# A fused attention and gMLP block on one core: a new hand-written order of steps, with c second on SyncE's queue, the query fold ahead of the value shift and late w_sp blocks

## The chip, the core and the metric

The kernel runs on one core of one Trainium2 chip. The metric is the device time of one execution in microseconds (us). The kernel before took 252.75 us, the median of three runs (252.35 to 254.44).

TensorE is written PE below, VectorE DVE, ScalarE ACT, GpSimd POOL; SP is SyncE, which in this kernel only issues DMAs. "ACTq" and "SPq" are the sequencers of ACT and SP, in which their DMA issues stand.

## What is computed

```python
mod = (silu(c) @ w_mod).reshape(1, 6, 1, 448)      # sa, ca, ga, sb, cb, gb
h = layernorm(x) * (1 + ca) + sa
x = x + ga * A(h)        # attention with 16 heads of 28
h = layernorm(x) * (1 + cb) + sb
x = x + gb * B(h)        # gMLP
# A(h): q, k, v = h @ wqkv; phi(t) = [softmax(t @ w_phi), softmax(-t @ w_phi)]
#       kv = phi(k)^T v ; z = sum phi(k) ; o = (phi(q) kv) / (phi(q) z + 1e-6) ; o @ wo
# B(h): z = gelu(h @ w_in); z1, z2 = halves of 896; z2 = layernorm(z2)
#       g = w_sp @ z2 + b_sp ; (z1 * g) @ w_out
```

x has 2048 rows of 448 in bf16; w_sp is 2048 x 2048, w_in 448 x 1792, w_out 896 x 448, w_mod 448 x 2688, and c is one row of 448.

## The kernel before

**Tiles.** The 2048 rows are 16 tiles of 128 rows. The 448 columns are 4 chunks of 112 (CB), so that a head never spans two chunks; the 896 columns of a half of w_in are 7 chunks of 128. PSUM is handed out as three banks of double size (A0, A1, A2) and two single ones (B0, B1); a step that takes a bank waits until all readers of what stood in it are done.

**The order.** `fast_path` defines some sixty small step functions and then runs one string, `ORDER`, word by word (895 words). A word is a step's name, its numbers, the engine behind a slash and the bank behind an @: `SCv:3/G` is value-row chunk 3 on POOL, `kM:0@B0` the key projection of tile 0 into bank B0. Letters stand for engines: V is DVE, S is ACT, G is POOL, Y is SP. No scheduler reorders anything: the order of the words is the order of the instructions on every engine's queue, and an instruction that waits holds back all that is queued behind it on its engine. DMAs share eight completion slots in the order of the words, so that each DMA also waits for the one issued eight DMAs before it.

```python
ENG = {"V": nc.vector, "S": nc.scalar, "G": nc.gpsimd, "Y": nc.sync}
for word in ORDER.split():
    word, _, slot = word.partition("@")
    word, _, en = word.partition("/")
    nm, _, arg = word.partition(":")
```

**The ramp (to about 28 us).** `du:n` is n matmuls of zeros, 128x256, that keep PE busy while loads are on their way (L686). `ct` turns c into columns (L697), `ce` is its silu, `csA` and `ccA` multiply it with the first two sections of w_mod (L721), `esA` and `ecA` bring the results into shift and scale columns (L728, L725). w_phi and the scale are folded into the key and query weights: `FT` transposes a weight on PE (L779), `ET` copies it out (L783, L785), `FS` and `FC` work out the shift row, `PF` multiplies with w_phi (L806) and `EP` writes the folded weight Wk or Wq with the scale applied (L753 on ACT, L757 on DVE). The value weights are not folded: `SHv` works out their shift row from the unscaled rows on PE (L735), then four `SCv` scale the rows in place, one per chunk (L753, L755, L757 for ACT, POOL, DVE; chunk 0 is read out of PSUM with the shift row). LN1 is `l1s` (statistics, L813), `l1e`, `l1r` (reciprocal root on POOL, L821) and `l1a` (the normalised row block, L824). The first four tiles are transposed on PE (`X` L837, `XE`), the others by DMA (`T1`, L829).

**The key stage (about 12 to 54 us).** Per tile: `kM` projects (L847), `kE` and `kF` are exp of plus and minus on ACT (L850), `vM` and `vC` the value rows (L855, L858), `kS`, `kR`, `kP` normalise the features on DVE and POOL (L861, L865, L868) and `kA` adds to the kv sum on PE (L878). `qM` projects two chunks of queries for 512 rows (L902), `qE` and `qF` are their exp (L907). `gr` and `ge` make the gate rows (L913, L916).

**The attention stage (about 54 to 109 us).** Per tile: `nM` multiplies query features with the kv sum (L930), `nX`, `nC`, `nS`, `nT`, `nA` divide (L938 to L956), `T2` transposes by DMA (L829), `wM` is the output projection (L966), `wR` adds x and sums the row, `wQ` sums the squares (L971, L978 on ACT, L973, L980 on DVE), `l2R`, `l2r`, `l2a` are LN2 (L986 to L999), and `T3` transposes the result by DMA into f_hT (L1004). `wN` is `wM` with one more matmul, of x with the identity (L964), so that ACT can read the sum out of PSUM. `dm:9,3` is nine small matmuls of zeros into the num bank (L935). `csB`, `ccB`, `SHw` and `SCw` prepare w_in as before the value weights.

**The gMLP.** `zM` is z2 = h @ w_in per tile (L1010), `zG` its GELU (L1014), `zQ`, `zR`, `zW`, `zN` its layer norm; `yM` and `yG` are z1, transposed, 512 rows a step (L1039, L1042). `W` loads and transposes 8 blocks of w_sp by DMA (L1047). From 139 us on w_sp @ z2 is done in a scheme with sums of blocks that saves products (`tT`, `sS`, `gM`, `P`, `d`, `x`: L1063 to L1106), with the output projection `oM` (L1120), its add `oE` (L1123) and the stores `oD` between. `ld:bsp` loads b_sp. `guard` and `read` test the range of the sums; the general path behind the test is not taken.

Of the kernel before, what the change touches and what calls it, by code (L numbers as in the profile page):

```python
# [486 lines left out]
def fast_path(tc, A_x, A_wqkv, A_w_phi, A_wo, B_w_in, B_w_sp, B_b_sp, B_w_out, c, w_mod, out, flag):  # L487
    nc = tc.nc
    S = A_x.shape[1]
# [77 lines left out]
    wv = aph.tile([P, KC, D], BF, name="f_wv")  # L567
# [281 lines left out]
    def kE(i, s):  # L849
        nc.scalar.activation(out=Er[i % NR][:, s, :], in_=ps["k" + str(i)][:, 0, 0:D], func=ACT.Exp, scale=1.0 - 2.0 * s)  # L850
# [73 lines left out]
    def nM(i, slot):  # L924
        t = ps["n" + str(i)] = bank(slot, "num")
        E = Eq[i // 8]
        o = (i % 8) * P
        for s in range(2):
            for cc in range(4):
                nc.tensor.matmul(t[:, s, cc * 120:(cc + 1) * 120], lhsT=E[0:CB, cc, s, o:o + P],  # L930
                                 rhs=KVbd[0:CB, s, cc, :, :].rearrange("p h d -> p (h d)"), start=True, stop=True)

    def dm(n, i):
        for _ in range(n):
            nc.tensor.matmul(ps["n" + str(i)][:, 1, 480:512], lhsT=zero[:, 0:P], rhs=zero[:, 0:32], start=True, stop=True)  # L935
# [12 lines left out]

# [12 lines left out]
    def wM(i, slot, with_x):  # L961
        t = ps["x" + str(i)] = bank(slot, "x1_ps")
        if with_x:
            nc.tensor.matmul(t[:, 0, 0:D], lhsT=ident[:], rhs=x_sb[:, i, :], start=True, stop=False)  # L964
        for cc in range(KC):
            nc.tensor.matmul(t[:, 0, 0:D], lhsT=oT[0:CB, i % 4, cc, :], rhs=wo_s[0:CB, cc, :], start=(cc == 0 and not with_x), stop=(cc == KC - 1))  # L966
# [261 lines left out]
```

## Time and profile before

| | us |
|---|---|
| median of 3 runs | 252.75 (252.35 to 254.44) |
| the profiled execution | 253.16 |
| its span in the profile | 251.3 |
| PE busy | 241.7 (96%) |
| DVE, POOL, ACT busy | 186.2 (74%), 119.1 (47%), 105.9 (42%) |
| PE idle before its first matmul | 1.24 |
| PE idle in gaps from there to 95 us | 3.9 |
| from the end of the last matmul to the end of the span | about 4 |

The granted clock of PE is full in all 40 slices of the span. An idle time stands in the profile in brackets, before the instruction that ended it, with what released it. The chain of waits is followed back from the last instruction, at each step to what released it, or else to the instruction before it on its engine. A matmul's duration in a row holds its pipelined end, so that neighbouring rows overlap: from one start to the next is its pitch.

### The profile page before, as it was taken

To read this page: it belongs to the slowest core of one execution; us is meant where nothing else is said; L and a number is where in the kernel's file an instruction comes from. 1 tells how busy PE (TensorE), PEld (TensorE's weight loads), DVE (VectorE), ACT (ScalarE), POOL (GpSimd) and SP (SyncE) were. 2 spreads that over 40 slices of the span, in tenths; PEclk is the share of its full clock that TensorE was granted. 3 is DMA by queue.
4 is the path that set the end of the run, shared out by engine and by line. 5 is a ranking of instruction groups with operands and counts; after the bars stand their busy time and mean duration, and the time that the engine had idled before them with its cause. 6 is when DMAs were issued, how large, how long until landed. Compare 5 with 4: busy or idle time off the path is not lost.

```text
span 251.3 us, 4227 instructions
## 1 busy us (share of the span) xinstructions
PE 241.7 (96%) x1550; PEld 127.1 (51%) x1550; DVE 186.2 (74%) x378; ACT 105.9 (42%) x219; POOL 119.1 (47%) x161
## 2 busy tenths in 40 slices
PE   8999998999989799999999999999999999999993
PEld 5865555576546454444444444444444444444451
DVE  4799999777999968874548999599976436644552
ACT  2498977735879658896897300000000000000000
POOL 3749997503568663486834064101119511034530
PEclk9999999999999999999999999999999999999999
DMA  7987569951588849789691977000001000101022
GB/s 181 275 231 173 97 144 200 233 141 21 103 164 113 158 85 183 122 146 221 121 179 28 172 133 77 0 0 0 3 0 37 0 3 1 55 0 37 21 92 68
DMA packets 68208, 25.23 MB, mean 100 GB/s; under 512 B 58129, under 2 KB 67602, under 8 KB 68178
## 3 DMA queue, kind: packets, MB, share of 16 engines
q1 hardware_dynamic: 64848, 20.78, 42.5%
q10 hardware_dynamic: 3330, 4.09, 5.9%
q8 instruction: 14, 0.23, 0.4%
q14 instruction: 16, 0.13, 0.2%
HBM read 8.87 MB, written 1.84 MB: 43 GB/s over the span
## 4 chain that ended last, share of the span: by engine, by line
PE 77%; DVE 11%; DMA 4%; POOL 3%; issue 2%; ACT 1%; POOLq 0%; DVEq 0%
PE g_ps L1085 29%; PE z_ps L1039 10%; PE z_ps L1010 9%; PE o_ps L1120 8%; PE g_ps L1106 5%; DMA f_hT<-f_xpad 4%; PE x_ps L966 3%; PE warm_ps L686 3%; DVE f_st L813 3%; PE q_ps L902 2%; PE v_ps L855 2%; DVE f_ar L950 2%; PE kvacc L878 2%; DVE f_ksum L861 2%; PE num L930 2%
## 5 line engine op out<-in xcount | busy, mean ns | idle before, releaser
L1094 DVE TENSOR_TENSOR f_zb<-g_ps,f_zb 128x512 f32<-128x512 f32 (+1 forms) x31 | 20.3, 669 | 17.5 <-PE g_ps L1085 17.1
L1085 PEld LDWEIGHTS <-f_z2n 128*128 128x128 bf16 x192 | 18.8, 98 | 22.5
L1101 POOL TENSOR_TENSOR f_z1T<-f_zb,f_z1T 128x512 bf16<-128x512 f32 (+1 forms) x11 | 11.9, 1102 | 35.0 <-DVE f_zb L1094 35.0
L1039 PE MATMUL z_ps<-f_hT,f_ar 112*128 112x512 bf16 x112 | 26.3, 379 | 1.3 <-DMA f_hT<-f_xpad 1.3
L1010 PE MATMUL z_ps<-f_ar,f_hT 112*128 112x448 bf16 (+1 forms) x128 | 26.5, 352 | 0.0
L1120 PE MATMUL o_ps<-f_wout,f_z1T 128*128 128x448 bf16 x112 | 22.5, 352 | 0.0
L1085 PE MATMUL g_ps<-f_ar 128*128 128x512 bf16 x96 | 22.2, 379 | 0.0
L1042 ACT ACTIVATE f_z1T<-z_ps,f_zb 128x512 bf16<-128x512 f32 x28 | 18.4, 683 | 6.7 <-PE z_ps L1039 6.7
L1101 POOL TENSOR_TENSOR f_z1T<-f_Sx,f_z1T 128x512 bf16<-128x512 f32 x6 | 7.1, 1182 | 27.2 <-DVE f_Sx L1094 27.2
L907 ACT ACTIVATE f_Eq<-q_ps 112x1024 bf16<-112x1024 f32 x16 | 16.1, 1036 | 6.5 <-PE q_ps L902 6.5
L1010 PEld LDWEIGHTS <-f_hT 112*128 112x128 bf16 (+1 forms) x128 | 12.2, 97 | 11.7 <-DMA f_hT<-f_xpad 0.3
L1039 PEld LDWEIGHTS <-f_ar 112*128 112x128 bf16 x112 | 10.9, 97 | 14.2 <-issue 1.8
L861 DVE TENSOR_REDUCE f_ksum<-f_E 128x32 f32<-128x896 bf16 x16 | 16.7, 1056 | 1.4 <-ACT f_E L850 1.4
L950 DVE TENSOR_TENSOR f_ar<-num,f_w 128x896 bf16<-128x896 f32 x16 | 16.9, 1084 | 0.4
L1014 ACT ACTIVATE f_zb<-z_ps 128x896 bf16<-128x896 f32 x16 | 14.6, 915 | 5.6 <-PE z_ps L1010 4.4
L850 ACT ACTIVATE f_E<-k_ps 128x448 bf16<-128x448 f32 x32 | 16.0, 556 | 1.7 <-PE k_ps L847 1.6
L1085 PE MATMUL g_ps<-f_Eq,f_z2n 128*128 128x512 bf16 x72 | 16.7, 379 | 0.0
L1120 PEld LDWEIGHTS <-f_z1T 128*128 128x128 bf16 x112 | 11.0, 98 | 10.7
L1123 DVE TENSOR_TENSOR f_xpad<-o_ps,f_x 128x448 bf16<-128x448 f32 x16 | 9.9, 621 | 8.0 <-PE o_ps L1120 7.9
L847 PE MATMUL k_ps<-f_Wk,f_hT 113*128 113x448 bf16 (+1 forms) x64 | 14.6, 352 | 0.8 <-DMA f_hT<-f_xpad 0.8
L902 PE MATMUL q_ps<-f_hT,f_Wq 113*128 113x512 bf16 (+1 forms) x64 | 15.0, 379 | 0.1
L1085 PEld LDWEIGHTS <-f_ar 128*128 128x128 bf16 x96 | 9.4, 98 | 11.2
(207 smaller groups left out, 483.1 us busy)
## 6 DMA issues: line engine op xcount, KB each, us to landing
out_dram<-f_xpad SPq DMA_DIRECT2D x16, 112.0 KB, 1.7
f_ar<-in_B_w_in_dram ACTq DMA_DIRECT2D x2, 784.0 KB, 5.3
f_wm<-in_w_mod_dram SPq DMA_DIRECT2D x3, 406.0 KB, 5.8
f_x<-in_A_x_dram SPq DMA_DIRECT2D x2, 448.0 KB, 8.7
f_wmg<-in_w_mod_dram ACTq DMA_DIRECT2D x2, 392.0 KB, 4.2
f_wout<-in_B_w_out_dram SPq DMA_DIRECT2D x1, 784.0 KB, 5.3
f_bsp<-in_B_b_sp_dram SPq DMA_DIRECT2D x1, 512.0 KB, 4.3
f_x<-in_A_x_dram ACTq DMA_DIRECT2D x1, 448.0 KB, 6.3
```

The lines of the kernel that those rows point to most:

```text
L850: nc.scalar.activation(out=Er[i % NR][:, s, :], in_=ps["k" + str(i)][:, 0, 0:D], func=ACT.Exp, scale=1.0 - 2.0 * s)
L861: nc.vector.tensor_reduce(out=ksum[:, i], in_=Er[i % NR][:].rearrange("p s (c f h) -> p (s c) h f", c=4, h=HP), axis=AX.X, op=ALU.add)
L902: nc.tensor.matmul(t[:, u, :], lhsT=Wq[0:KR[m], m, cc * CB:cc * CB + P], rhs=hT[0:KR[m], 4 * st:4 * st + 4, m, :], start=(m == 0), stop=(m ...
L907: nc.scalar.activation(out=Eq[st // 2][0:CB, 2 * c2:2 * c2 + 2, s, (st % 2) * 512:(st % 2 + 1) * 512], in_=ps["q" + str(n)][0:CB, :, :], f ...
L950: nc.vector.tensor_tensor(out=tr[i % 2][:], in0=numv(i)[:, :, :, 0:DH], in1=wr[i // 2 % 2][:, i % 2].unsqueeze(3).to_broadcast([P, 2, H, D ...
L1010: nc.tensor.matmul(t[:, hf, 0:D], lhsT=hT[0:KR[m], i, m, :], rhs=win_s[0:KR[m], m, FH + hf * D:FH + (hf + 1) * D], start=(m == 0), stop=(m ...
L1039: nc.tensor.matmul(t[:, 0, :], lhsT=win_s[0:CB, m, fc * P:(fc + 1) * P], rhs=hT[0:CB, 4 * st:4 * st + 4, m, :], start=(m == 0), stop=(m == ...
L1042: nc.scalar.activation(out=stage_b()["z1T"][:, fc, st * 512:(st + 1) * 512], in_=ps["y%d_%d" % (st, fc)][:, 0, :], func=ACT.Gelu_apprx_tan ...
L1085: nc.tensor.matmul(g, lhsT=sta[:, m, :], rhs=mov[:, m, :], start=(m == 0 and i in (1, 6, 7)), stop=(m == 7), skip_group_check=True)
L1094: nc.vector.tensor_tensor(out=o, in0=x, in1=y, op=ALU.add)
L1101: eng.tensor_tensor(out=z, in0=T[r][:, c0:c1], in1=z, op=ALU.mult)
L1120: nc.tensor.matmul(ps["o" + str(t)][:, 0, 0:D], lhsT=later["z1T"][:, FO[n], t * P:(t + 1) * P], rhs=wout_s[:, FO[n], :], start=(n == 0), s ...
```

## The change

ORDER is written anew, with 893 words; the last 87 (from `P:1,0,x` for the lower half on) are the same. Beside it, `dm` goes, and so does the word `wN`: `wM` takes an engine, and adds the identity matmul where this is ACT.

```diff
-du:2@A1 ld:wk/S ld:x1/Y l1s:1 l1e:1,2/V l1r:1,2 tbl du:3@A2 ld:c/S du:3@A0 m1/G ld:x0/Y ld:wsa/Y m2a/V du:3@B1 du:14@A1 m4 ld:phi/Y du:3@B0 l1s:0 ct@B0
+tbl du:8@B1 m2b/V ld:wk/Y du:3@A2 m2a/V du:11@A1 ld:c/Y ct@B0 ld:x1/S l1s:1 ld:x0/S l1s:0 m1/G ld:phi/Y ce:1 m3 FTk:1@B1 ce:2 l1e:1,2/G ld:wsa/Y du:2@A0
...
-SHv@A1 SCv:0/S EPk:2/V EPk:3/V kM:0@B0 l1a:3/V SCv:2/V FTq:0@B1 ld:x3/Y SCv:1/S ETq:0/V kE:0 FTq:1@A1
...
-SCv:3/G FCq/S EPq:1/S XE:3/S vM:1@A0
+kM:1@B1 FTq:1@A2 ETq:1/V ld:x3/Y FTq:0@B0 ETq:0/V kM:0@A0 kF:1 FSq@A2 FCq/V kE:1 kS:1 PFq:1@B0 scb kF:0 kE:0 l1r:2,4 l1a:2/G l1a:3/G l1s:4 X:2@B1 SHv@A1 PFq:2@A2
+SCv:1/G EPq:1/S XE:2/S l1s:6 PFq:0@B0 SCv:2/G X:3@A0 l1s:5 kM:2@B1 SCv:0/S XE:3/S l1s:7 ld:x4/Y l1s:9 EPq:0/S SCv:3/G l1e:4,8/G l1s:11 kS:0 vM:2@A1 vM:3@B0
...
-    def dm(n, i):
-        for _ in range(n):
-            nc.tensor.matmul(ps["n" + str(i)][:, 1, 480:512], lhsT=zero[:, 0:P], rhs=zero[:, 0:32], start=True, stop=True)
...
-"wM": lambda i, slot: wM(i, slot, False), "wN": lambda i, slot: wM(i, slot, True),
+"wM": lambda i, slot, eng: wM(i, slot, eng is nc.scalar),
```

What moves, by stage (82 steps also change their engine; the new file's line numbers are 43 higher up to L935 and 39 higher behind it):

- **Loads.** On SP's queue: wk, c, phi, wsa, wca, x2, wq, wv, x3, x4, then wmgb and wmga; x1 and x0 stand on ACT's queue. Before, wk and c stood on ACT's queue and x1, x0 first on SP's. x5 now stands on ACT's queue behind the exp of key tile 2; win0 and wout are issued by ACT at the end of the key stage, win1 by SP.
- **Warm-up.** 22 matmuls of zeros ahead of `ct` where there were 28, and 35 in all where there were 41.
- **Ramp.** Key tile 1 comes ahead of tile 0. The query weights are transposed and their fold is begun ahead of `SHv`, which moves behind `kM:0`. Value chunks 1, 2 and 3 are all scaled on POOL (before: ACT, DVE, POOL), and `vM:2` is the first value projection.
- **Attention.** Five tiles take the identity matmul (0, 1, 2, 3, 5) where seven did (0, 1, 2, 3, 4, 10, 11). `SHw:2` moves to where `dm` stood. Four of the `SCw` stand on ACT between the queries' exps, where one did; `nM:13` and the output projections of tiles 10 to 14 come later, that of tile 14 just ahead of `zM:8`.
- **z2 and z1.** `T3:14,16`, the last transpose of LN2's rows, is issued behind more work of POOL and SP. Most blocks `W:1,x` and the load of b_sp move behind `T3:10,12`, six blocks `W:2,x` into the stage with the products, and `yG:2,1` with them; `tT:1,2` moves to POOL and `tT:4,0` to DVE.

Three places show the move. **POOL's queue in the ramp**, from the normalised rows of LN1's first tiles on (f_wv are the value rows, f_xpad normalised rows, f_phik key features). Before:

```order
L824 TENSOR_SCALAR f_xpad<-f_x,f_nm_143,f_rs_142 128x4x112
L755 TENSOR_SCALAR f_wv<-f_wv,f_ca_136 112x448
L673 COPY f_scb<-f_scol 112x512
L817 TENSOR_SCALAR f_rs_142<-f_mv_141 128x4
L818 TENSOR_SCALAR f_nm_143<-f_mv_141 128x4
L821 TENSOR_TENSOR f_rs_142<-f_rs_142,f_mhalf 128x4
L824 TENSOR_SCALAR f_xpad<-f_x,f_nm_143,f_rs_142 128x4x112 x4
L868 TENSOR_TENSOR f_phik<-f_E_123,f_kr_129 128x896
```

and now:

```order
L798 TENSOR_SCALAR f_wv<-f_wv,f_ca_136 112x448 x3
L860 TENSOR_SCALAR f_rs_142<-f_mv_141 128x4
L861 TENSOR_SCALAR f_nm_143<-f_mv_141 128x4
L864 TENSOR_TENSOR f_rs_142<-f_rs_142,f_mhalf 128x4
L867 TENSOR_SCALAR f_xpad<-f_x,f_nm_143,f_rs_142 128x4x112 x4
L911 TENSOR_TENSOR f_phik<-f_E_123,f_kr_129 128x896
```

Three value chunks stand in a row ahead of LN1's next tiles, where one did; the copy of f_scb has gone ahead of them.

**ACT's queue in the attention stage**, from the second exp of query chunk 5 (the first row) to `wR` of tiles 2 and 3 (f_Eq are the exps, f_Sx copies from num, f_ar<-sh_ps and f_ar<-f_ar rows of w_in being scaled, f_x and f_ar<-f_x the steps `wR` and `wQ`). Before:

```order
L907 ACTIVATE f_Eq<-q_ps 112x2x512
L753 ACTIVATE f_ar<-sh_ps,f_cb_83 113x448
L938 COPY f_Sx<-num 128x32
L971 ACTIVATE f_x,f_s_88<-x_ps 128x448
L938 COPY f_Sx<-num 128x32
L978 ACTIVATE f_ar,f_s_89<-f_x 128x448
L971 ACTIVATE f_x,f_s_88<-x_ps 128x448
L978 ACTIVATE f_ar,f_s_89<-f_x 128x448
L907 ACTIVATE f_Eq<-q_ps 112x2x512
L938 COPY f_Sx<-num 128x32 x2
L907 ACTIVATE f_Eq<-q_ps 112x2x512
L971 ACTIVATE f_x,f_s_88<-x_ps 128x448 x2
```

and now:

```order
L950 ACTIVATE f_Eq<-q_ps 112x2x512
L1010 ACTIVATE f_x,f_s_88<-x_ps 128x448
L796 ACTIVATE f_ar<-sh_ps,f_cb_83 113x448
L977 COPY f_Sx<-num 128x32 x2
L1017 ACTIVATE f_ar,f_s_89<-f_x 128x448
L1010 ACTIVATE f_x,f_s_88<-x_ps 128x448
L796 ACTIVATE f_ar<-f_ar,f_cb_83 112x896 x2
L950 ACTIVATE f_Eq<-q_ps 112x2x512
L977 COPY f_Sx<-num 128x32 x2
L796 ACTIVATE f_ar<-sh_ps,f_cb_83 113x448
L950 ACTIVATE f_Eq<-q_ps 112x2x512
L1010 ACTIVATE f_x,f_s_88<-x_ps 128x448 x2
```

Two scalings of 112x896 and a second one of 113x448 have come between the queries' exps; the second `wQ` has gone to DVE.

**SP's queue in the z2 stage**, around the last transposes of LN2's rows (f_hT<-f_xpad are `T3`, f_Eq, f_wsp and f_hT<-in_B_w_sp blocks of w_sp). Before:

```order
L1004 DMA_TRANSPOSE f_hT<-f_xpad 128x8x128
L633 DMA f_bsp<-in_B_b_sp_dram 128x2048
L1004 DMA_TRANSPOSE f_hT<-f_xpad 128x8x128
L1047 DMA_TRANSPOSE f_Eq<-in_B_w_sp_dram 128x8x128
L1004 DMA_TRANSPOSE f_hT<-f_xpad 128x8x128
L1047 DMA_TRANSPOSE f_Eq<-in_B_w_sp_dram 128x8x128 x2
L1004 DMA_TRANSPOSE f_hT<-f_xpad 128x8x128
L1047 DMA_TRANSPOSE f_Eq<-in_B_w_sp_dram 128x8x128
L1047 DMA_TRANSPOSE f_wsp_85<-in_B_w_sp_dram 128x8x128
```

and now:

```order
L1043 DMA_TRANSPOSE f_hT<-f_xpad 128x8x128 x2
L1086 DMA_TRANSPOSE f_Eq<-in_B_w_sp_dram 128x8x128 x3
L1043 DMA_TRANSPOSE f_hT<-f_xpad 128x8x128
L1086 DMA_TRANSPOSE f_Eq<-in_B_w_sp_dram 128x8x128 x3
L1086 DMA_TRANSPOSE f_wsp_85<-in_B_w_sp_dram 128x8x128 x2
L676 DMA f_bsp<-in_B_b_sp_dram 128x2048
L1086 DMA_TRANSPOSE f_hT<-in_B_w_sp_dram 128x8x128 x2
```

Ahead of the last transpose of LN2's rows stand three w_sp blocks where two did, and b_sp has gone from ahead of three of these transposes to behind all of them.

49 lines of the change are left out of this document (45 added, 4 removed).

## The prediction

> **What bounds the kernel now.** I read the busy shares and the chain of waits first, then PE's waits, then stretches of the span.
>
> ```profile
> PE 241.7 (96%) x1550; PEld 127.1 (51%) x1550; DVE 186.2 (74%) x378; ACT 105.9 (42%) x219; POOL 119.1 (47%) x161
> PE 77%; DVE 11%; DMA 4%; POOL 3%; issue 2%; ACT 1%; POOLq 0%; DVEq 0%
> 98.00:139.00 41.00, 41.00 (x204) 19.51 (x203) 27.69 (x77) 33.99 (x68) 24.97 (x44) 1.00 0.73 138
> 139.00:188.00 49.00, 49.00 (x229) 22.21 (x228) 43.28 (x55) 2.42 (x4) 11.94 (x6) 1.00 0.31 49
> ```
>
> PE is the bound: 77% of the chain is its own, and in the stretches from 98 to 188 us (columns: length, then busy time of PE, of its weight loads, DVE, ACT, POOL, the granted clock, the DMA share, GB/s) it is busy in every microsecond. There a new order gains nothing; it can only lose. What can be gained is PE work left out and PE's waits, and these are few:
>
> ```profile
> PE z_ps L1039 <- DMA f_hT<-f_xpad: 1.3, 1, 1.3
> PE warm_ps L686 <- DVE f_zero L644: 1.2, 1, 1.2
> PE num L930 <- DVE f_ar L950: 1.2, 3, 0.6
> PE k_ps L847 <- DMA f_hT<-f_xpad: 0.8, 1, 0.8
> PE num L930 <- ACT f_zb L1014: 0.7, 1, 0.7
> ```
>
> (Columns: total, times, longest.) The wait for zeros opens the program and stays. The other four, 3.9 us by their gaps, lie between 42 and 95 us, three of them in the attention stage. Together with the PE work removed below they are nearly all that the change can win.
>
> **The start.** c is issued second on SP's queue, where x0 was; x1 and x0 take the first places on ACT's, which wk and c had, so that all four are issued within the same first microsecond as before and cost nothing.
>
> ```profile
> 1.24 5.24 PE L686 MATMUL warm_ps<-f_zero 128*128 128x256 bf16 x28 [1.24 <-DVE f_zero L644]
> 6.53 0.31 PE L697 MATMUL ct_ps<-f_one,f_c_row 1*112 1x1 bf16 x4
> 1.24:3.24 2.00, 2.00 (x10) 1.44 (x11) 1.00 0.63 144
> 7.87:8.76 0.89, 0.89 (x8) 0.68 (x8) 1.00 1.12 275
> 5.62 0.63 DVE L813 BATCH_NORM_STATS2 f_st<-f_x 128x6 f32<-128x448 bf16 x1
> 7.30 0.58 POOL L821 TENSOR_TENSOR f_rs<-f_rs,f_mhalf 128x1 f32<-128x1 f32 x1
> 10.96 0.16 DVE L725 TENSOR_SCALAR f_ca<-cf_ps 112x4 f32<-112x4 f32 x1
> 12.71 0.55 PE L847 MATMUL k_ps<-f_Wk,f_hT 113*128 113x448 bf16 x2
> ```
>
> The first warm-up matmuls come at 2.00/10 = 0.20 us each, later ones at 0.89/8 = 0.11. Of the 28 ahead of `ct` the last six go, and these are of the later kind: 6 x 0.11 = 0.65 us, so that `ct` could start at 5.9 instead of 6.53. Charged at the mean of the first row (5.24/28 = 0.19) it would be 1.1 us. The Trainium skill, "TensorE: Matmul & The Clock Gate", section "What's actually happening", has the warm-up last for a time (some 3.4 us) and not for a number of matmuls; the two rates above agree, and by it too the six that go are cheap ones. Little of the 0.65 reaches the key projection. x0 is now transposed first; its statistics can't begin before it lands (5.6 in the DVE row), and behind the root on POOL (7.30 + 0.58 = 7.9) and the row block on DVE (0.39) it is ready at about 8.3, where PE arrives at 7.9 (two sets of transposes at 0.46 and eight warm-ups from 5.9 on). From there X, csA, PF, X, FS and ccA bring the scale column to about 10.5 (10.96 in the row), and the last of three folds of Wk in a row on ACT, at the pitch of 0.53 that two rows below have, is done at about 12.4. Key tile 1 then ends at 12.6, where before tile 0, with the value shift done too, ended at 12.71 + 0.76 = 13.47. The shift's 0.76 is still to do: I take **-0.2 us**.
>
> **The value rows.** The four chunks are needed by the first value projection.
>
> ```profile
> 11.95 0.92 PE L735 MATMUL sh_ps<-f_wv,f_Ga 112*128 112x448 bf16 x4
> 12.91 0.63 ACT L753 ACTIVATE f_wv<-sh_ps,f_ca 113x448 bf16<-113x448 f32 x1 [0.33 <-PE sh_ps L735]
> 13.44 0.66 ACT L753 ACTIVATE f_wv<-f_wv,f_ca 112x448 bf16<-112x448 bf16 x1
> 13.08 1.08 POOL L755 TENSOR_SCALAR f_wv<-f_wv,f_ca 112x448 bf16<-112x448 bf16 x1
> 13.35 0.39 DVE L824 TENSOR_SCALAR f_xpad<-f_x,f_nm,f_rs 128x448 bf16<-128x448 bf16 x1
> 20.04 2.80 POOL L824 TENSOR_SCALAR f_xpad<-f_x,f_nm,f_rs 128x448 bf16<-128x448 bf16 x4
> 20.03 0.63 DVE L813 BATCH_NORM_STATS2 f_st<-f_x 128x6 f32<-128x448 bf16 x1
> ```
>
> Before, ACT, DVE and POOL shared them, and all were scaled 2 us ahead of need. Now chunks 1 to 3 follow one another on POOL behind `SHv`. PE issues, from the end of `SHv` to `vM:2`, two PF (0.21 each), an X (0.23) and `kM:2` (0.76), 1.4 us, and meets chunk 3 another 0.57 later: cover of 2.0 us. POOL's rows give two prices for such a block of 448: 2.80/4 = 0.70 while DVE ran statistics, 1.08 once, while DVE ran a scaling out of SBUF. Three in a row are 2.1 or 3.2 us, and with the hand-over (some 0.2) the stall is 0.4 or 1.4. DVE's queue beside the three holds statistics and a sum over features, so I take 0.70 and **+0.4**, and keep +1.4. Queued behind these on POOL are LN1's tiles 4 to 7, which the fifth key tile needs 8 us later: covered.
>
> **The key stage.** k_ps waited 0.77 us for the transposes of tiles 12 to 15. Their LN1 rows on POOL and DVE come earlier among the words than the key tiles that use them did, so I take all of it, **-0.77**, and keep 0 (x5 is issued later, behind `kF:2`).
>
> **The attention stage up to the first z2 tile.** The nine small matmuls go, and of seven identity matmuls two.
>
> ```profile
> L964 PE MATMUL x_ps<-f_x,f_ident 128*128 128x448 bf16 x7 | 2.5, 353 | 0.0
> 67.09 0.38 PE L935 MATMUL num<-f_zero 128*128 128x32 bf16 x9
> 70.03 0.59 PE L930 MATMUL num<-f_ar,f_Eq 112*128 112x120 bf16 x8 [0.61 <-DVE f_ar L950]
> 54.00:78.00 24.00, 22.77 (x233) 13.73 (x231) 20.05 (x51) 16.86 (x41) 12.42 (x20) 1.00 0.48 91
> 65.18 0.63 ACT L753 ACTIVATE f_ar<-sh_ps,f_cb 113x448 bf16<-113x448 f32 x1 [0.32 <-PE sh_ps L740]
> 81.04 1.04 ACT L753 ACTIVATE f_ar<-f_ar,f_cb 112x896 bf16<-112x896 bf16 x1
> 66.67 0.58 ACT L978 ACTIVATE f_ar<-f_x 128x448 bf16<-128x448 bf16 x1
> 76.40 1.04 ACT L907 ACTIVATE f_Eq<-q_ps 112x1024 bf16<-112x1024 f32 x1
> ```
>
> `dm` is 0.40 by its row. It stood in front of a num that then waited 0.61 for DVE: taken out alone it would only lengthen that wait, but `SHw:2` (four matmuls, 0.76) moves into its place. So **-0.40**, and the three waits of num for DVE, 1.2 together, go by the order of the tiles if nothing else is late: **-1.17**. PE's lead at the first z2 tile would be 0.2 - 0.4 + 0.77 + 0.40 + 1.17 = 2.1 us.
>
> It meets ACT there. `zM:0` takes the bank of the last query chunk and waits for its second exp, 76.40 + 1.04 in the row. Ahead of it ACT now has two scalings of 1.04 and one of 0.63 more, and one square (0.58 and 0.18 for reading its sum out) less: 2.71 - 0.76 = 1.95 us. From 54 to 78 us ACT idled 24.00 - 16.86 = 7.1 us, so all of it could be hidden; but most of that idle time ends with PE's queries, ahead of the added scalings, and those stand in front of exps that other work waits for. I take the pessimistic end, **+1.95** (0 at the other), a lead of 0.2 at `zM:0`.
>
> **Behind it.** The wait of z_ps for a transpose (1.31) was for LN2's rows of tiles 2 and 3. In the new order PE has 5.4 us of work from `zM:0` to that use, and ACT's squares, POOL's moments and root and the transpose need about 5.7 from there: **-1.0**. The one num that now takes a bank behind a GELU (tile 15) has two z1 steps, 1.7 us, of cover: **-0.68**. Two identity matmuls at a pitch of 0.19 (448 columns each, as the k_ps rows: 0.76 for four): **-0.38**. A new wait: `nM:13` takes the bank of the output projection of tile 8, and DVE reads that only behind a division and two adds.
>
> ```profile
> 73.24 2.08 DVE L950 TENSOR_TENSOR f_ar<-num,f_w 128x896 bf16<-128x896 f32 x2
> 75.35 0.39 DVE L956 TENSOR_TENSOR f_ar<-f_ar 128x448 bf16<-128x448 bf16 x1
> 80.00 0.61 DVE L973 SCALAR_TENSOR_TENSOR f_x<-x_ps,f_x 128x448 bf16<-128x448 f32 x1
> ```
>
> On DVE 1.04 + 2 x 0.39 + 0.7 = 2.5 us, on PE two projections and a num, 1.9: **+0.6** (0 to 1).
>
> **The z2 stage and the products.** The last transpose of LN2's rows is the one that comes late.
>
> ```profile
> 108.20 1.68 PE L966 MATMUL x_ps<-f_ar 112*128 112x448 bf16 x8
> 126.01 2.75 PE L1039 MATMUL z_ps<-f_hT,f_ar 112*128 112x512 bf16 x12
> 122.67 1.23 SPq L1004 DMA_TRANSPOSE f_hT<-f_xpad  x1
> 120.00 1.07 DVE L980 SCALAR_TENSOR_TENSOR f_ar<-f_zb 128x896 bf16<-128x896 bf16 x1
> f_hT<-f_xpad SPq DMA_TRANSPOSE x15, 3.3
> ```
>
> Before, 18 us lay between the projection of tile 14 and the first z1 step that needs it. Now PE has six z2 tiles at 1.52, four z1 steps at 0.86 and the guard between them, 12.65 us. DVE's queue there is the read and the two squares of tiles 14 and 15 (2.1), the moments (0.75), one normalised z2 tile (0.5), a square of 896 (1.07) and the two row blocks, about 6.5 with the waits; with 3.3 for the transpose 10 to 12 us. It fits: **0**, up to +2 where POOL's root stands behind zR, zW and zN. The load of b_sp now has some 7 us to its use and took 4.3; the blocks `W:2,x` are used more than ten us behind their place; the last 87 words are the same: 0 each.
>
> **The sum.** -0.2 + 0.4 - 0.77 - 0.40 - 1.17 + 1.95 - 1.0 - 0.68 - 0.38 + 0.6 = -1.65 us, so that the profiled 253.16 us (251.3 of span, 1.9 around it) would be 251.5. It lies 0.4 above its runs' median; for the median, 252.75 - 1.65 = **251.1 us**.
>
> **The rivals.** *All gaps close.* ACT's idle time swallows the scalings and `nM:13` comes in time: -1.65 - 1.95 - 0.6 = -4.2, 248.5 us. For it: 7.1 us of idle; against it: three engines would have to be in time at every tile.
>
> *ACT sets the pace* (the other side). If ACT's queue ends last not only at `zM:0` but on to 98 us, as its GELUs, squares and scalings stand in one line, then the work taken from PE and the waits of the attention stage give nothing, since PE would wait for ACT in their place: -0.2 + 0.4 - 0.77 + 1.95 + 0.6 = +2.0, 254.7 us. It decides once the second exp of query chunk 7 ends more than about 0.5 us later than its 77.4 of now. Against it: ACT's 16.86 busy us in 24.
>
> *The late transpose.* If POOL's root holds the row blocks of tiles 14 and 15 up by 2 us beyond the cover, PE stands in the stage that has no gap now: -1.65 + 2.0, 253.1 us.
>
> *POOL and DVE in each other's way.* The row of 1.08 is 0.38 longer than 0.70, just what the DVE scaling within it took (0.39). If that recurs for all three value chunks: -1.65 + 1.0, 252.1 us. The Trainium skill, "SBUF — State Buffer", section "Who interferes with whom", has DVE's copies and scalings out of SBUF, but not its sums over features, able to lock POOL out for a whole instruction; by that the rows above agree, and the case turns on what DVE runs at that moment.
>
> **How the numbers follow.** My sum 0.40, all gaps close 0.22, ACT 0.20, late transpose 0.10, POOL 0.08. The likeliest alone would give 249.4 to 252.6 (the middle of the ACT term to the upper price of the value rows). The range of 8 in 10 reaches into the ends on both sides: 248.2 to 254.8. One per cent, 2.5 us, is about what a measurement of this kernel can tell from no change. Faster than 250.2: the low three tenths of the sum (0.12), all gaps (0.22), a fourth of POOL (0.02), 0.36. Slower than 255.3: four tenths of ACT (0.08), a fifth of the transpose (0.02), 0.10. Within: 0.54.
>
> **What would show it.** PE's first `ct` near 5.9; an idle piece of 0.3 to 0.6 before the first v_ps, released by POOL; none before k_ps at 42; the second exp of query chunk 7 near 77.3 and z_ps released by ACT there; no num waiting for DVE by more than 0.2 before it; PE full from 98 to 188 us of now, all of it 1 to 2 us earlier. I am wrong if PE shows a gap over 1 us behind 98 us, if the value rows cost over 1 us, or if the gaps of the attention stage come back under new releasers.

## The result, and the profile after

| | before | after |
|---|---|---|
| median, us | 253.59 of 4 (252.35 to 254.44) | 249.31 of 4 (248.69 to 250.34) |
| profiled execution, us | 253.16 | 249.40 |
| its span, us | 251.3 | 247.6 |
| PE busy, us | 241.7 | 240.5 |

The ratio is 0.985, with an interval of 0.9813 to 0.9888: 1.5% faster. A second set gave 249.51 (6 runs, 249.09 to 250.47) against 253.2: 0.9857 (0.983 to 0.9885). The forecast had the sign and the bound, and the time lies within its range (248.2 to 254.8), but of 3.76 us between the two profiled executions it foresaw 1.65, and 249.31 lies just below the 249.4 to 252.6 of its likeliest case.

First the busy shares and the chain of waits of the page after:

```profile
PE 240.5 (97%) x1533; PEld 126.8 (51%) x1533; DVE 182.5 (74%) x369; ACT 104.8 (42%) x217; POOL 116.3 (47%) x175
PE 85%; POOL 6%; ACT 3%; DVE 2%; DMA 1%; issue 1%; POOLq 0%
```

DVE's share of the chain fell from 11% to 2%, PE's rose from 77% to 85%. PE's waits after (columns: in total, times, longest):

```profile
PE warm_ps L729 <- DVE f_zero L687: 1.2, 1, 1.2
PE q_ps L945 <- ACT f_Eq L950: 0.6, 1, 0.6
PE x_ps L1005 <- DVE f_x L1012: 0.3, 1, 0.3
PE g_ps L1145 <- DVE f_z2n L1072: 0.2, 1, 0.2
PE warm_ps L729 <- DVE f_Wk L800: 0.2, 1, 0.2
```

All four waits that the prediction listed are gone, the one for a transpose included (z_ps, 1.31). New are 0.58 for ACT early in the queries, 0.26 for DVE (x_ps), 0.24 within the products (g_ps) and 0.24 in the ramp (warm_ps, for DVE's work on a key weight). The same in stretches from milestone to milestone, first of before, then of after (length, then PE busy and its matmuls):

```profile
54.08:77.64 23.56, 22.32 (x229) 1.00 0.47 89
77.64:139.41 61.77, 59.78 (x332) 1.00 0.74 135
139.41:236.34 96.93, 96.93 (x458) 1.00 0.18 33
```

```profile
53.23:75.55 22.32, 21.72 (x222) 13.29 (x219) 19.18 (x51) 17.66 (x40) 8.73 (x17) 1.00 0.48 119
75.55:134.87 59.32, 59.06 (x330) 29.87 (x329) 43.00 (x110) 47.66 (x103) 40.88 (x81) 1.00 0.80 142
134.87:232.38 97.51, 97.27 (x458) 44.52 (x456) 68.90 (x95) 1.87 (x4) 27.22 (x17) 1.00 0.23 41
```

The stretches end at the first queries behind the kv sum, the first z2 tile, the first product and the last output projection. Against the terms of the sum:

| stretch | forecast | measured |
|---|---|---|
| start to the first of these queries | -0.57 | 54.08 to 53.23: -0.85 |
| to the first z2 tile | +0.38 (of it ACT +1.95) | 23.56 to 22.32: -1.24 |
| to the last output projection | -1.46 | 158.70 to 156.83: -1.87 |
| tail | 0 | 14.96 to 15.22: +0.26 |
| all | -1.65 | -3.70 |

The third row's pieces add up to it: -1.31 (z_ps), -0.68 (num behind a GELU), two identity matmuls at 0.19, and +0.26 and +0.24 for the new waits, -1.87. That they fit so well is partly chance: the stretch ahead of the first product is 0.34 shorter than its pieces say (61.77 to 59.32), the one behind it 0.34 longer (96.93 to 97.51). The second is the row in which the forecast failed: with ACT's term at 0 and the new wait of 0.58 its terms give -0.99, and the rest is a little less PE work (22.32 to 21.72, of which `dm` has 0.40).

### The profile page after: what moved, and what is told of

Its sections match the earlier page's. It is cut to its first block, busy times and chain, and to the rows that moved or that the text cites. A ratio compares the mean times of both kernels' runs of the same rounds, so it can differ in the third digit from the quotient of the medians.

```text
span 247.6 us, 4188 instructions
## 1 busy us (share of the span) xinstructions
PE 240.5 (97%) x1533; PEld 126.8 (51%) x1533; DVE 182.5 (74%) x369; ACT 104.8 (42%) x217; POOL 116.3 (47%) x175
## 4 chain that ended last, share of the span: by engine, by line
PE 85%; POOL 6%; ACT 3%; DVE 2%; DMA 1%; issue 1%; POOLq 0%
PE g_ps L1124 29%; PE o_ps L1159 9%; PE z_ps L1049 7%; PE q_ps L945 6%; PE k_ps L890 5%; PE v_ps L898 5%; PE g_ps L1145 5%; PE z_ps L1078 4%; PE x_ps L1005 4%; PE kvacc L921 3%; PE warm_ps L729 3%; PE num L973 2%; POOL f_zv L1035 1%; DMA f_hT<-f_xpad 1%; DVE f_z2n L1072 1%
## 5 line engine op out<-in xcount | busy, mean ns | idle before, releaser
L1140 POOL TENSOR_TENSOR f_z1T<-f_Sx,f_z1T 128x512 bf16<-128x512 f32 x6 | 8.0, 1332 | 39.3 <-DVE f_Sx L1133 39.3
L1159 PEld LDWEIGHTS <-f_z1T 128*128 128x128 bf16 x112 | 11.0, 98 | 10.7
L1005 PE MATMUL x_ps<-f_ar 112*128 112x448 bf16 x64 | 14.1, 352 | 0.3 <-DVE f_x L1012 0.3
```

The source lines that it names most:

```text
L1140: eng.tensor_tensor(out=z, in0=T[r][:, c0:c1], in1=z, op=ALU.mult)
L1159: nc.tensor.matmul(ps["o" + str(t)][:, 0, 0:D], lhsT=later["z1T"][:, FO[n], t * P:(t + 1) * P], rhs=wout_s[:, FO[n], :], start=(n == 0), s ...
```

## The experiments

All of them are compared with the kernel before on the same chip, whose median was 253.2 in each set.

### One part of the order at a time

**The new order up to the end of the key stage, the old one behind it** (h_abb). ORDER is cut at `KV:0`; a few words that would stand twice or be missing (loads and blocks of w_sp, and the like) are put where their own order has them. The next two are made in the same way.

```diff
 # ORDER, cut at KV:0; ahead of it the new words
-KV:0/V KV:1/V KZ:0 ld:win0/S qM:3@A2 KZ:1 nM:0@A1 qE:3
+KV:0/V KV:1/V qM:3@A2 KZ:0 KZ:1 nM:0@A1 wos:1/V qE:3
...
```

> The new order up to the end of the key stage (all words ahead of KV:0), the old order behind it. Stage-by-stage theory: PE is the bound and each stage's gain is its own, so the first query projection behind the kv sum (q_ps at 54.1 before, 53.2 in the new order) starts near 53.2, the rest is as before: 0.9 us faster than before, span about 250.4. Rival, the lead is lost again: the attention stage of the old order waits for VectorE and transposes, so an earlier start is given back there; then the time is that of before within 0.3 us, with longer waits of num. Rival, the stages gain only together: no gain at the seam either.

Measured: 252.16 (10 runs, 251.83 to 253.49), 0.9974 (0.9953 to 0.9995). The queries start at 53.47, 0.61 earlier than before, and the three waits of num for DVE are back with 1.2 in all. z_ps waits 0.86. The ramp and the key stage alone are worth about 1 us, of which 0.45 is that shorter wait of z_ps, behind the cut.

**The old order up to there, the new one behind** (h_baa).

```diff
 # ORDER, cut at KV:0; ahead of it the old words
-KV:0/V KV:1/V qM:3@A2 KZ:0 KZ:1 nM:0@A1 wos:1/V qE:3
+KV:0/V KV:1/V KZ:0 ld:win0/S qM:3@A2 KZ:1 nM:0@A1 qE:3
...
```

> The old order up to the end of the key stage, the new order behind it. Stage-by-stage theory: q_ps behind the kv sum near 54.1 as before, then the new order's 22.3 us to the first z2 tile (23.6 before) and 59.3 to the first product (61.8 before): 2.8 us faster than before, span about 248.5. Rival, the new attention order needs the lead that the new ramp gives: less than half of that, with waits of num or z_ps that the new order did not show.

Measured: 251.78 (10 runs, 251.02 to 253.57), 0.9964 (0.9941 to 0.9987). From the first queries to the first z2 tile it takes 22.32 us (54.52 to 76.84), just as the whole new order does, so this stretch's gain is that of its own words. But 1.4 us of gain in all is half of the 2.8 expected. PE's timeline shows two waits, both for DMA transposes:

```profile
42.73 0.93 PE L890 MATMUL k_ps<-f_Wk,f_hT 113*128 113x448 bf16 x4 [0.99 <-DMA f_hT<-f_xpad]
83.34 1.02 PE L1082 MATMUL z_ps<-f_hT,f_ar 112*128 112x512 bf16 x4 [0.94 <-DMA f_hT<-f_xpad]
```

The first is 0.2 longer than before; the second stands in words that are the same as in the new order, which has no wait at this place (80.94 in its row below). The two halves are worth 1.04 + 1.42 = 2.46 us, the whole 253.2 - 249.51 = 3.69. Most of the gap of 1.2 can be placed in the traces. Of z_ps's wait the halves take 0.45 and 0.37, the whole takes 1.31: 0.49 is missing. The queries start 0.61 earlier in h_abb and 0.44 later here (0.23 of it by k_ps), 0.85 earlier in the whole: 0.68 is missing.

**Only the words from the first z2 tile on** (h_bba). In it x is added twice in tile 4 and not in tile 5.

```diff
 # ORDER, cut at zM:0; ahead of it the old words, then one more wR
-zM:0@A2 nA:7/G l2R:2,4/G SCw:3,0/V wR:4/S gt nS:4 nT:9
+wR:5/S zM:0@A2 gt nA:7/G l2R:2,4/G nC:9 nS:4 nT:9 nT:8
...
```

> The old order up to the first z2 tile, the new order behind it (the steps done on one side only of the seam are kept once). Stage-by-stage theory: z2 starts near 77.6 as before, and 59.3 us later the products start (61.8 before), less 0.6 that the products lose: 1.9 us faster than before, span about 249.5. Rival, the waits that are gone there (z_ps for a transpose 1.31, num for the GELU 0.68) were set by work ahead of the first z2 tile: they come back, and the gain is about 0.4, the two identity matmuls.

Measured: 252.42 (10 runs, 251.33 to 253.38), 0.9961 (0.9935 to 0.9987). The stretch to the first product takes 60.1 us, between 61.77 and 59.32: z_ps does not wait, but x_ps waits 0.67 and 0.29 for DVE. So this part gives some 0.8, less than the 1.9 expected and more than the rival's 0.4, and the attention stage, h_baa less h_bba, some 0.6, with the 0.94 that h_baa's z_ps waits counted against it.

### The disputed term: does ACT have room?

**The three scalings back on DVE** (scw_back).

```diff
-SCw:2,1/S qM:6@A2 SCw:0,0/S
+SCw:2,1/V qM:6@A2 SCw:0,0/V
...
-SCw:0,2/S qF:6
+SCw:0,2/V qF:6
```

> The new order with three scalings of w_in's rows (chunks 0,0, 2,1 and 0,2) back from ScalarE on VectorE, where they were before; 1.56 us of VectorE, 2.7 us of ScalarE. Theory now: in the old order VectorE paced the attention stage (num waited for it three times), and the gain there is that ScalarE does these rows in its idle time. Then waits of num for VectorE come back and z2 starts 0.5 to 1.5 us later than in the new order (75.6). The recorded sum (ScalarE's added work on the path, +1.95): z2 starts earlier, by 0.6 (its one wait of q_ps for ScalarE) up to 2 us. Third, both have room: within 0.2 us.

Measured: 253.4 (10 runs, 253.22 to 254.29), 1.0019 (1.0 to 1.0038): the whole gain is gone. PE's timeline, and DVE's just ahead of it:

```profile
71.18 0.59 PE L973 MATMUL num<-f_ar,f_Eq 112*128 112x120 bf16 x8 [1.59 <-DVE f_ar L989]
72.18 0.98 PE L973 MATMUL num<-f_ar,f_Eq 112*128 112x120 bf16 x8 [0.41 <-DVE f_ar L989]
```

```profile
67.71 0.81 DVE L800 TENSOR_SCALAR f_ar<-f_ar,f_cb 112x896 bf16<-112x896 bf16 x2 [0.81 <-PE sh_ps L783]
68.44 0.92 DVE L984 TENSOR_TENSOR f_dn<-f_cr 128x32 f32<-128x32 f32 x1
```

On DVE the two scalings take only 0.81, but they wait another 0.81 for `SHw:2`, and the division of the next tiles is queued behind them. The waits of num for DVE are back, 2.0 us of them. Moving these blocks to ACT is what let the waits of num close. The first z2 tile starts at 80.43, 4.5 later than in the new order's second profile, where 0.5 to 1.5 was expected. The waits are 2.0 of it, the queries' later start 0.7 (54.30), and some 1.7 (half of 3.4) comes from the granted clock, which in this execution was halved for 3.4 us there (see the end). Runs with a mean clock of 0.998 to 1.000 took 253.3 to 253.8 too, so that the clock does not carry the loss. Where those spent what the waits don't explain no profile shows.

**More work on ACT** (act_plus): four copies of 128x448 ahead of `qF:6`, nothing depends on them.

```diff
+    def aj(n):
+        for _ in range(n):
+            nc.scalar.activation(out=junk[:, 0:D], in_=junk[:, 0:D], func=ACT.Copy)
...
-SCw:0,2/S qF:6
+SCw:0,2/S aj:4 qF:6
```

> The new order with four added copies of 128x448 on ScalarE ahead of the second exp of query chunk 6, some 1.9 us, as much again as the new order put there. Theory now: in the new order ScalarE runs without idle time from 66 us on and ends the last exp at 75.48, when z2 starts at 75.55; the added 1.9 us come out at the first z2 tile almost whole (77.0 to 77.5) and at the end (1.5 to 1.9 us slower than the new order). Rival, that ScalarE with 42% of the span busy has room: less than 0.5 us. Had the recorded term (+1.95 for the first 1.95 us on this queue) been right, ScalarE would have been late already and the whole 1.9 would come out again, with z2 waiting for ScalarE.

Measured: 253.36, the median of nine runs (252.01 to 254.33; a tenth, at 511 us, is left out), 0.9999 (0.9972 to 1.0025). ACT's row of the copies and PE's row behind them:

```profile
71.34 2.42 ACT L979 ACTIVATE f_ar<-f_ar 128x448 bf16<-128x448 bf16 x4
```

```profile
74.72 2.27 PE L946 MATMUL q_ps<-f_hT,f_Wq 113*128 113x512 bf16 x8 [2.09 <-ACT f_Eq L951]
```

PE takes nearly all of the copies as a wait: the exp behind them ends at 74.68 and releases it. The first z2 tile starts at 80.65, where 77.0 to 77.5 was expected; a halved clock has a part in this as well (see the end). That ACT had no room left shows in the new order too, by its ACT rows:

```profile
73.39 1.00 ACT L950 ACTIVATE f_Eq<-q_ps 112x1024 bf16<-112x1024 f32 x1
74.30 0.26 ACT L977 COPY f_Sx<-num 128x32 f32<-128x32 f32 x2
74.44 1.04 ACT L950 ACTIVATE f_Eq<-q_ps 112x1024 bf16<-112x1024 f32 x1
```

and PE's:

```profile
75.55 1.69 PE L1049 MATMUL z_ps<-f_ar,f_hT 113*128 113x448 bf16 x8
80.94 1.03 PE L1078 MATMUL z_ps<-f_hT,f_ar 112*128 112x512 bf16 x4
```

The last exp ends at 75.48 and the z2 tile that takes its bank starts at 75.55, with no wait. The change filled ACT's idle time to the brim and not beyond. Two stretches of the new order, 66 to 72 and 72 to 78 us (PE, its loads, DVE, ACT, POOL), say the same:

```profile
66.00:72.00 6.00, 5.98 (x43) 3.25 (x41) 5.72 (x14) 5.95 (x13) 4.57 (x9) 1.00 0.41 78
72.00:78.00 6.00, 6.00 (x50) 3.61 (x49) 5.76 (x14) 5.86 (x15) 5.47 (x11) 1.00 0.50 98
```

PE, DVE and ACT are each busy for 5.7 or more of 6 us. The one experiment puts 1.6 us of scaling and waiting back on DVE, the other 2.4 us on ACT, and either loses what was won.

### Where the transpose's wait went

The wait of z_ps for a transpose was 1.31 before, 0.94 in h_baa and none after, though LN2's words are the same in the last two. The next five runs look for what decides it.

**The new order again** (after_again), for a second profile.

```diff
 # no edit
```

> The new order once more, on the chip of the variants of it that follow: about 3.8 us faster than before (ratio 0.985 so far), first z2 tile near 75.5, the products near 134.9.

Measured: 249.51 (6 runs), 0.9857 (0.983 to 0.9885); the queries start at 53.58, the first z2 tile at 75.90, and z_ps does not wait.

**28 warm-ups ahead of `ct`, as before** (du28).

```diff
-tbl du:8@B1 m2b/V
+tbl du:14@B1 m2b/V
```

> The new order with the six warm-up matmuls back, 28 ahead of ct. If warm-up matmuls are plain TensorE work on the path, 0.65 us slower than the new order at the first key projection. But x0's statistics and root set the first transpose (xt_ps at 8.5 in all runs of the new ramp, with or without an idle time ahead of it): then TensorE is later only by what exceeds that, 0.3 to 0.6 us where the clock rises late and nothing where it rises early.

Measured: 250.7 (4 runs, 250.47 to 251.4), 0.9899 (0.9867 to 0.993), 1.2 more than the new order beside it. In the profiled execution (span 249.3 against 247.8) the queries are 0.34 later, as expected (53.92); what was not expected is the wait of z_ps, which is back with 1.30. The DMA view from 79.4 to 82 us (40 slices of 0.065 us) shows a transfer that stops:

```profile
GB/s 32 126 449 224 209 209 197 209 205 169 138 43 24 8 0 0 0 0 0 0 0 0 0 0 0 0 0 4 8 8 8 12 8 8 12 8 12 8 12 59
q8 instruction: 1, 0.02, 3.9%
```

In the new order, from 78.7 to 80.5 (slices of 0.045 us), it runs through:

```profile
GB/s 6 85 148 199 228 210 222 222 233 199 222 210 222 193 222 239 182 228 199 210 210 188 199 228 182 199 199 217 154 80 51 34 370 0 0 0 0 0 0 0
q8 instruction: 1, 0.02, 4.2%
```

In both stretches one packet of 16 KB lies on the queue called "instruction", of which the span has 14. It is the one slice above 300 GB/s (370 GB/s over 0.045 us are 16.6 KB). In du28 it comes 0.1 us after the transfer began, and from 0.85 us after its start the transfer all but stands still (0 to 12 GB/s) for 1.6 us. In the new order it comes at the transfer's end, 1.4 us after its start, and nothing stands still. My theory from here on: these packets come with the number of PE's instructions, and one that comes early in a transpose delays it by a microsecond or more. The rival: the later start of du28 decides.

**Six small matmuls in a wait of PE, at no cost in time** (fetch_early): `dm` again, 128x32, ahead of `qM:4`, where PE waits for ACT anyway.

```diff
+    def dm(n, i):
+        for _ in range(n):
+            nc.tensor.matmul(ps["n" + str(i)][:, 1, 480:512], lhsT=zero[:, 0:P], rhs=zero[:, 0:32], start=True, stop=True)
...
-nT:0 qM:4@A2
+nT:0 dm:6,1 qM:4@A2
```

> The new order with six more matmuls of 128x32 zeros (into unused columns of a num bank) just ahead of qM:4, where TensorE waits 0.58 us for ScalarE anyway; at 0.04 each they cost no time there. They only push what TensorE still has to fetch as instructions by twelve places. Theory: the 16 KB instruction packets on queue q8, one about every 27 us of TensorE work, stop a DMA transpose that is under way for 1.2 to 1.6 us; in the new order such a packet comes at 80.8, just after the transpose of LN2's tiles 2 and 3 has landed. Here it comes some 1.3 us earlier, into that transpose: z2 still starts near 75.6 to 75.9, the first z1 step waits 0.7 to 1.4 us for a DMA as it did before the change, and the time is 0.7 to 1.3 us above the new order's. Rival, that the transpose was late for another reason (the later start of the whole): no wait, the new order's time.

Measured: 250.86 (5 runs, 250.18 to 251.96), 0.9897 (0.9855 to 0.994). The first z2 tile starts at 75.88, as in after_again (75.90), and still:

```profile
82.41 1.02 PE L1082 MATMUL z_ps<-f_hT,f_ar 112*128 112x512 bf16 x4 [0.96 <-DMA f_hT<-f_xpad]
```

Its packet comes 0.75 us after the start of the transfer.

**28 warm-ups ahead of `ct`, but six fewer behind** (du28_same): the count of matmuls at the attention stage is that of the new order again.

```diff
-tbl du:8@B1 m2b/V
+tbl du:14@B1 m2b/V
...
-l1a:0/G du:6@A2 X:0@B0
+l1a:0/G X:0@B0
```

> 28 warm-up matmuls ahead of ct as in the earlier run, but without the six later ones (du:6), so that TensorE has as many instructions ahead of the attention stage as the new order. That earlier run was 1.2 us slower, of it 0.34 in the ramp and 1.30 in a wait of the first z1 step for a DMA transpose. Theory of the instruction packets: the place of the packet is that of the new order again, no such wait, and the time is within 0.4 us of the new order's (249.3 to 250.0). Rival, that the later start of all that follows made the wait: the ramp is as late as in the earlier run and the wait of about 1.3 stays, 250.7.

Measured: 249.97 (5 runs, 249.34 to 251.19), 0.9873 (0.9831 to 0.9914); the first z2 tile at 75.76, and no wait:

```profile
81.16 1.03 PE L1078 MATMUL z_ps<-f_hT,f_ar 112*128 112x512 bf16 x4
```

The packet is at the end of the transfer, 1.4 us after its start. Both runs came out as the theory said. du28_same does not test the rival by itself, as its start was not late (queries at 53.44). fetch_early does: its z2 starts when that of the new order does, and the wait is there. And two runs in this document start z2 late without that wait: h_bba at 77.47 and mended, below, at 77.21; their packets come 2.6 us behind the issue of the transpose, as the new order's does. So the rival falls.

**The old order without `dm`** (old_late), which should bring the packet of the old order late enough.

```diff
-nS:2 dm:9,3 SCw:0,0/V
+nS:2 SCw:0,0/V
```

> The old order without its nine matmuls dm (0.40 us of TensorE). As plain TensorE work they are worth nothing: num waits for VectorE right behind them, 0.61 now and 1.0 then, and z2 starts at 77.6 as before. By the theory of the instruction packets it is worth 0.7 to 1.3 us all the same: nine pairs of instructions fewer bring the packet that came at 81.0, within the transpose of tiles 2 and 3, to about 82.6, when the transpose is through, and the wait of the first z1 step (1.31) goes or shrinks: span 250.0 to 250.6. Rival without such packets: span 251.2 to 251.4.

Measured: 254.55 (11 runs, 253.07 to 256.28), 1.0045 (1.0015 to 1.0074): slower. As forecast, `dm` taken out alone gives nothing: num waits 1.04 in its place, and the stretch up to the first z2 tile takes 23.56 us as before. But z_ps still waits 0.89, so the gain hoped for there is missing. The DMA view from 83 to 85 us (slices of 0.05 us; the transfer began at 82.1) has the reason:

```profile
GB/s 205 543 184 184 138 169 220 164 88 31 0 0 36 72 36 15 15 20 5 0 10 5 10 10 5 10 10 10 10 10 10 5 10 10 10 31 241 276 297 287
```

The packet (543) comes at 83.1, 4.0 us behind the first z2 tile (79.07), where it was 2.7 behind it before: it did move, by 1.3, but it is still only 1.0 into the transfer, which then stops from 83.5 to 84.7. The mechanism stands; how far the packet had to move was misjudged. The ramp, whose words are unchanged, was slower: 28 warm-ups took 6.01 us (5.24 before), and the queries started at 55.51. In this execution the warm-up matmuls go at 6 to 7 a microsecond up to 7.2 us, where before they did so up to 5.2; but the median of eleven runs is slower too, and why is open.

### Two mendings

**Two new waits mended at once** (mended), 0.58 of q_ps and 0.24 within the products: the work of `FB` into the wait of q_ps, with win1 loaded earlier for it, and `tT:1,2` on POOL behind the z2 rows of tiles 14 and 15.

```diff
-csB@B0 W:0,1 ld:win1/Y
+csB@B0 esB W:0,1
...
-nT:0 qM:4@A2
+nT:0 FB@B0 qM:4@A2
...
-nX:3 FB@B1 wos:1/V
+nX:3 wos:1/V
...
-zQ:14/S tT:1,2/G yG:3,0
+zQ:14/S yG:3,0
...
-zR:14,16/G zW:14,16 zN:14/V
+zR:14,16/G zW:14,16 tT:1,2/G zN:14/V
```

(`ld:win1/Y` now stands behind `kF:15`, and `esB` behind `csB`.)

> The new order with its two remaining waits in the middle taken on: the bias matmuls FB (0.68 us of TensorE) go ahead of the query projection that waits 0.58 for ScalarE's exp, with what they need (win1 loaded behind kF:15, the shift column esB right behind csB), and GpSimd's moments of tiles 14 and 15 go ahead of tT:1,2 (2.1 us), which held up the last normalised z2 tiles (0.24). Theory (TensorE is the bound, ScalarE just in time at the first z2 tile): the second gives 0.24; the first gives 0.58 at the query projection, but ScalarE's queue up to the first z2 tile gains only what the earlier query brings it, so 0.3 to 0.6 in all at the products, 0.4 to 0.8 us. Rival: ScalarE's and VectorE's queues are the pace there, and only the 0.24 shows.

Measured: 250.29 (6 runs, 249.55 to 251.19), 0.9886 (0.9857 to 0.9916), 0.8 more than the new order beside it. PE's waits:

```profile
PE x_ps L1003 <- ACT f_zb L826: 1.3, 1, 1.3
PE fb_ps L789 <- DMA f_ar<-in_B_w_in_dram: 0.6, 1, 0.6
```

The 0.58 for ACT became 0.59 for win1's load, and `FB` in bank B0 made the next user of that bank wait for ACT's copy of it, which stands behind exps. The wait of 0.24 within the products did go. Where a gain of 0.4 to 0.8 was expected, 0.8 is lost.

**Only the second of the two** (mended2).

```diff
-zQ:14/S tT:1,2/G yG:3,0
+zQ:14/S yG:3,0
...
-zR:14,16/G zW:14,16 zN:14/V
+zR:14,16/G zW:14,16 tT:1,2/G zN:14/V
```

> The new order with only the second of the two edits tried: GpSimd's moments of tiles 14 and 15 ahead of tT:1,2. The wait of the products for the last normalised z2 tiles (0.24) goes, as it did there; 0.2 to 0.3 us faster than the new order, too little for the timing to tell, to be seen in the places of the rows.

Measured: 249.01 (5 runs, 248.72 to 251.14), 0.985 (0.9802 to 0.9897). The stretch from the first product to the last output projection is 96.93 us again:

```profile
135.07:232.00 96.93, 96.40 (x448) 44.59 (x456) 68.39 (x93) 1.87 (x4) 25.50 (x16) 1.00 0.23 42
```

It is the best of all the kernels here, but its 0.3 to 0.5 below the new order's medians can't be told from them by the times; the stretch in the trace (97.51 to 96.93) is what shows the gain.

## Why the prediction was right, and where its sum failed

**What bounds the kernel: right.** PE did, and its waits between 42 and 95 us were what could be won. All closed; the new ones sum to 1.3 us, and none is over 0.6.

**The start, -0.2: near.** `ct` starts at 6.04 (forecast 5.9). x0 is indeed the next to be late: the first transpose starts at 8.53 (8.3), and the key projection at 12.10 against 12.71. That `ct` came out so near is in part luck: the 22 warm-ups took 3.86 to 4.88 us in the profiles (see the end).

**The value rows, +0.4: none.** POOL's row and the first value projection of the new order:

```profile
16.07 1.87 POOL L798 TENSOR_SCALAR f_wv<-f_wv,f_ca 112x448 bf16<-112x448 bf16 x3 [0.25 <-PE sh_ps L778]
```

```profile
17.58 1.69 PE L898 MATMUL v_ps<-f_wv,f_hT 113*128 113x448 bf16 x8
```

Three scalings take 1.87, 0.62 each (priced 0.70), while DVE runs a sum over features until 16.30 and statistics behind it; v_ps does not wait. (The prediction's own terms, 2.1 + 0.2 - 2.0, give 0.3 and not 0.4.) The price of 1.08 for the meeting with a DVE scaling did not occur, so that rival was not put to the test. Its row had two DVE scalings out of SBUF within it, 0.39 from 13.35 and 0.64 from 13.65 on, and not one; the prediction had "just what the DVE scaling within it took". The Trainium skill, "SBUF — State Buffer", section "Who interferes with whom", has DVE's sums over features never contend with POOL, and the trace agrees; that the statistics did not hold POOL up is the measured 0.62.

**k_ps, -0.77: right in size,** but h_baa (0.99, with the old words) shows it to move by some tenths.

**dm and num, -0.40 and -1.17: right.** old_late shows that `dm` alone gives nothing, scw_back that the waits of num close only because the scalings left DVE's queue.

**ACT, +1.95: the step that failed.** "I take the pessimistic end, +1.95 (0 at the other)." It was 0 at that place; the 0.58 of ACT's at another (q_ps behind `qF:3`) has no scaling ahead of it. The reason given against hiding was that most of ACT's idle time ends with PE's queries, ahead of the added scalings. Of the 7.0 us that ACT idled in the kernel before, from the first queries to its last exp, 4.9 do lie ahead of 66 us. But 2.2 lie behind it, as ACT's rows of before show:

```profile
69.46 1.02 ACT L907 ACTIVATE f_Eq<-q_ps 112x1024 bf16<-112x1024 f32 x1 [0.83 <-PE q_ps L902]
71.66 0.18 ACT L938 COPY f_Sx<-num 128x32 f32<-128x32 f32 x1 [0.81 <-PE num L930]
```

That is the place into which the scalings went, and it is more than 1.95. The new order leaves 0.1 of it: ACT is busy for 17.66 us of the 22.32 from the first queries to the first z2 tile, and for 5.95 and 5.86 of 6 us from 66 us on (above). The forecast judged the idle time as one whole. It also counted against old start times: ACT's last exp now ends 22.25 us behind the first queries, 23.36 before, since PE's work comes earlier once PE no longer waits for DVE. Two of the prediction's signs failed, the idle piece before the first v_ps (above) and the second exp of query chunk 7 near 77.3 with z_ps released by ACT there: it ends at 75.48, and z_ps does not wait. That the reading was close, though, act_plus shows: 2.4 us more on ACT, and 2.1 come out as a wait.

**z_ps, -1.0: -1.31,** for the reason given (LN2's rows are in time) and one that was not seen: the transfer must also miss an instruction packet. That it does is luck of the matmul count, which nobody chose for it. Had it not, 0.9 to 1.3 us would have come back, and the result would have been near the 250.7 and 250.9 of du28 and fetch_early.

**nM:13, +0.6: none;** its place is another, 0.26 for DVE's reading of an output projection. **The GELU's wait and the identities, -0.68 and -0.38: right.** **The late transpose, 0: right;** it is issued at 115.55, and what was mispriced is behind it, 0.24 for a z2 row that waits on POOL's `tT:1,2`, with 0.3 more in the products; both are gone in mended2.

Of the rivals, "all gaps close" (248.5 us) is what happened, within 0.8. It was set against with "three engines would have to be in time at every tile": they are, at the first z2 tile by a tenth of a microsecond. "ACT sets the pace" is what act_plus builds. What is only argued: that the new order's ACT moved forward because PE's num waits closed (scw_back, where they are back, fits). What stays open: old_late's ramp, and where scw_back's unprofiled runs lose their time.

## What to carry to other kernels

When a wait on the bounding engine is removed, don't price new work on a third engine by the sum of that engine's old idle time: find the idle pieces that lie where the work goes, lay the queue out again from the new start times, as some of these pieces hang on the same wait, and look at how full each engine is in the six microseconds around the place. When three engines are full at once the order has no slack, and some 2 us on either of the two others cost nearly 4, of which the profiled waits are 2. A gain that rests on a transfer's landing may hang on the number of instructions issued ahead of it, so measure such a kernel with a few more and a few fewer matmuls before believing it.

## What the runs showed of the hardware

**Instruction packets and transposes.** On queue q8, "instruction", 14 packets of 16 KB pass in a span of 248 us. In all fourteen profiles of this case the sixth of them comes when PE has started 728 to 737 matmuls, at times from 79.59 to 85.16 us; the new order and du28, with six warm-ups more, both have 728. In six profiles it comes at most 2.1 us behind the issue of that DMA transpose, which is from 0.4 us ahead of the transfer to 1.0 us into it (before, h_abb, h_baa, du28, fetch_early, old_late). There the transfer stood still for 1.0 to 1.6 us, and PE waited 0.86 to 1.31. In the other eight it comes 2.6 us or more behind the issue, at the transfer's end or later, and z_ps did not wait. Six more matmuls ahead brought the packet 0.7 to 1.3 us forward against the transpose. How a packet stops a transpose no run shows; pauses of 0.6 us occur in transfers without one too.

**The clock of PE.** Both times that PE stood still for about 2.0 us within 3.4 us in the attention stage, the granted clock was half for 3.4 us right behind this or 1.4 us later. In act_plus (length, PE busy, granted clock) and in scw_back:

```profile
76.10:79.50 3.40, 3.40 (x22) 0.50 0.59 113
```

```profile
72.20:75.60 3.40, 3.40 (x16) 0.50 0.40 75
```

In act_plus the runs whose mean clock was 0.999 took 252.0 and 252.2, those of 0.992 or 0.993 (one such stretch: half of 3.4 us in 252 is 0.007) 252.7 to 253.6, those of 0.982 to 0.986 (two or more; the profiled one had another in the ramp) 253.9 to 254.3. So the ACT work itself cost 2.6 us over the new order's 249.5, and each slow stretch about 1 more.

Behind the ramp, waits of 1.3 us (before, du28, mended) or of 1.04 and 0.40 close together (old_late) did not do this. In the ramp less was enough. The clock was half there too in both executions, in scw_back from 10.7 to 14.1 us (columns: length, PE, its loads, DVE, ACT, POOL, granted clock):

```profile
12.00:14.00 2.00, 2.00 (x10) 1.03 (x9) 1.65 (x7) 1.07 (x2) 0.23 (x1) 0.50 1.10 332
```

Ahead of it the first transpose had waited 1.05, in act_plus 0.76; in fetch_early a wait of 0.87 at the same place was not followed by a half clock. So the length of a wait alone does not decide it, and what does is open.

The Trainium skill, "TensorE: Matmul & The Clock Gate", section "What's actually happening", has the clock fall back after an idle window of some 3.4 us that runs freely; the length of the slow stretch agrees with it, but here a window of which PE was idle for some 2 us, and in the ramp for less, was enough.

**The warm-up.** How long the same matmuls take ahead of `ct` differs from run to run: 22 took 4.88 us in the new order and 3.86 in scw_back, whose words there are the same, so that `ct` starts at 6.04 or 5.03. At first 6 to 7 of them go in a microsecond; in scw_back 12 do from 4.2 us on, in the new order all 22 go at the first pace. The earlier start gains nothing, as x0's normalised rows are not there: the first transpose waits 1.05 us in scw_back.
